# Layer A's third and fourth value projections as seven Strassen products, with sums of x and weights made ahead

## The chip, the cores and the metric

One core of one Trainium2 chip runs the whole program. The metric is the device time of one execution in microseconds (us). The kernel before was timed in 3 runs: median 1818.2 us, from 1813.79 to 1818.61. One more execution was profiled; all durations of instructions come from that one.

## The reference

Two attention layers, A and B, stand side by side; their outputs are concatenated. Each has S = 2048 positions, D = 1024 features, 32 heads of 32, all in float32:

```
qkv = x @ wqkv                      # 2048x1024 @ 1024x3072
q, k, v = heads of qkv
A: each query sees 8 keys, at distances 0, 2, .., 14
B: each query sees the 256 keys up to itself
out = softmax(q k^T / sqrt(32)) v   # per head
return concat(a_out @ wo_A, b_out @ wo_B)
```

The change touches the part `v = x @ wqkv[:, 2048:]` of layer A.

## The kernel before

**Units.** Each layer is cut into 4 units of 512 positions, so there are units 0 to 7. Units 0 to 3 are layer B (dense blocks of scores), units 4 to 7 layer A. Layer A's positions are sorted into even and odd ones first, so a query's 8 keys are neighbours: a window. `U` is 8 and `DU`, the first unit of layer A, is 4.

**Numbers in two parts.** Every operand of the large matrix products is split into a high part, rounded to the matmul's fp32r format, and a low part that holds the rest. A product is three matmuls: high by high, high by low, low by high (`TERMS`). `Stream` loads the operands as a fixed list of items of 512 KB through `NRAW` = 3 landing tiles (`raw`, issued by POOL at line 173), and splits each one: ScalarE or VectorE writes the high part (lines 218 and 221), VectorE the low part (line 224). An item's split sends off the load three items further on.

**Work of one unit.** For each of 8 slots `s` there is one q and one k tile (`qk_items`, line 586: 2 x 8 x 3 = 48 matmuls of 512 columns). Between them stand the value projections (`v_items`, line 654) in three parts (`VPARTS`): part 0 makes the value features of slots 0 to 3 with 96 matmuls of 512 columns; parts 1 and 2 those of slots 4 and 5, and of 6 and 7, with 96 matmuls of 256 columns each. `V_SLOTS` puts the parts behind slots 0, 5 and 7. While part 2 runs, the next unit's x is loaded and split (`x_items`). Values stay in the SBUF tiles `vbuf`, one for each part. Layer B's output projections stand in units 1 to 5 (`o_items`, line 714).

**Output of layer A.** The two units 4 and 5, and then 6 and 7, are taken together, and the output projection over their rows is seven Strassen products instead of eight block products (`product`, line 773, 48 matmuls of 512 columns each): the rows are two halves (the two units), the contraction has two halves, and the outputs have two halves. Sums of blocks are made by `background` tasks: SyncE loads blocks into `r` tiles (line 841), VectorE adds (line 846), SyncE stores the sums to DRAM (line 852), from where `Stream` loads them like any weight. `weight_sums` makes the 4 weight sums of layer A's `wo`, `output_sums` those of the attention outputs `od`.

**Attention of a window.** `window` has two steps on TensorE: scores (line 923) and values (line 984). Between them VectorE masks, takes maxima and sums, and transposes (lines 931 to 961), and ScalarE spreads the result into `wide` (lines 970 and 973). SyncE copies q and k rows into seats in `pbuf` (line 506). PSUM has 3 banks for the large products (`rg`, tiles `g`), 4 for scores (`s`) and 1 for values (`o`).

**What sets the order.** All engines run their instructions in the order in which the program is written. That order comes from a planner in the program: `Clock` keeps estimated times, and the last loop of the function picks from four lists (`aux`, `twos`, `ones`, `gemm`) what can start first. A wait that the planner did not foresee holds everything behind it on that engine.

## Time and profile before

| | |
|---|---|
| median of 3 runs | 1818.2 us |
| profiled execution, whole | 1818.1 us |
| its span, first to last instruction | 1816.4 us |
| TensorE busy | 1789.4 us, 99% |
| VectorE busy | 1262.0 us, 69% |
| ScalarE busy | 924.4 us, 51% |
| mean granted TensorE clock | 0.995 |

The span is 1.7 us shorter than the execution, and the profiled execution is 0.1 us below the median, so a sum made on the trace can be set beside the median as it stands. In the trace, layer A's units 6 and 7 run from about 1337 to 1657 us, and the fourteen output products from 1657 to 1812 us. A busy TensorE in these views is one on which some matmul is under way.

### The profile page before, as it was taken

The numbers are of one execution on the slowest core, as the hardware profiler recorded it, in microseconds if no ns is written. First come the engines' busy times: TensorE is split into PE (matmuls) and PEld (weight loads), VectorE is DVE, ScalarE is ACT, GpSimd is POOL, SyncE is SP. The second block draws the span as 40 slices with busy tenths as digits, with TensorE's granted clock in tenths as the row PEclk, the third lists the DMA queues.
The fourth block names the chain that finished last, engine by engine and source line by source line (L and its number), as shares of the span: only waits on it lengthen the run. The fifth ranks groups of instructions, "written<-read, shape, count | busy, mean of one in ns | idle before, by whom it ended". The sixth has DMA issues, their size and how long they took to land.

```text
span 1816.4 us, 38617 instructions
## 1 busy us (share of the span) xinstructions
PE 1789.4 (99%) x14730; PEld 1465.3 (81%) x14730; DVE 1262.0 (69%) x2790; ACT 924.4 (51%) x2301; POOL 410.1 (23%) x950
## 2 busy tenths in 40 slices
PE   9999999999999999999999999999999999999999
PEld 6787878888777788778887788888888887888887
DVE  6677876768867769777677566646755766557866
ACT  5556466555655565656555344423542544446342
POOL 2313323222242223333224300101010011002220
PEclk9999999999999999999999999999999999999999
DMA  7354664544646555454545343536753674348984
GB/s 239 114 142 136 183 168 139 167 139 137 183 139 177 146 144 170 134 166 128 160 110 164 106 150 119 164 123 213 249 173 113 221 250 137 120 144 297 311 265 145
DMA packets 129241, 303.61 MB, mean 167 GB/s; under 512 B 16160, under 2 KB 31520, under 8 KB 129056
## 3 DMA queue, kind: packets, MB, share of 16 engines
q0 software_dynamic: 45216, 164.65, 28.7%
q1 hardware_dynamic: 73472, 116.56, 22.8%
q10 hardware_dynamic: 10368, 19.93, 3.0%
q8 instruction: 117, 1.92, 0.4%
q14 instruction: 68, 0.56, 0.1%
HBM read 189.79 MB, written 44.04 MB: 129 GB/s over the span
## 4 chain that ended last, share of the span: by engine, by line
PE 91%; DMA 3%; ACT 2%; DVE 2%; issue 1%; SPq 0%; POOL 0%; ACTq 0%; DVEq 0%; POOLq 0%
PE g L586 37%; PE g L654 18%; PE g L714 10%; PE g L773 8%; PE s L1172 5%; PE s L1089 5%; PE o L1219 5%; PE s L923 2%; PE o L984 2%; DMA r<-od 2%; DMA raw<-xs 1%; ACT wide L970 1%; ACT s L1099 0%; DVE w L224 0%; DVE r L846 0%
## 5 line engine op out<-in xcount | busy, mean ns | idle before, releaser
L586 PE MATMUL g<-x,w 128*128 128x512 f32 x3072 | 773.0, 396 | 2.8 <-ACT x L218 2.6
L586 PEld LDWEIGHTS g<-x,w 128*128 128x128 f32 x3072 | 568.1, 189 | 114.5 <-issue 6.8
L654 PE MATMUL g<-w,x 128*128 128x256 f32 (+1 forms) x2304 | 393.7, 322 | 0.5 <-issue 0.3
L224 DVE TENSOR_TENSOR w<-raw,w 128x512 fp32r<-128x512 f32 x518 | 339.4, 697 | 51.8 <-ACT w L218 45.1
L654 PEld LDWEIGHTS g<-w,x 128*128 128x128 f32 x2304 | 334.5, 192 | 28.8 <-issue 1.6
L1099 ACT ACTIVATE s<-s,nm 128x384 f32<-128x384 f32 (+2 forms) x512 | 274.4, 537 | 101.8 <-DVE nm L1094 101.6
L1094 DVE CUSTOM_DVE_ANT_0 s<-s,mask_d 128x384 f32<-128x384 f32 (+2 forms) x512 | 261.7, 554 | 88.1 <-PE s L1089 87.4
L1158 POOL TENSOR_SCALAR_AFFINE_SELECT pbuf<-pbuf 128x128 f32<-128x128 f32 (+1 forms) x606 | 220.1, 391 | 326.2 <-ACT pbuf L1179 324.8
L1179 ACT ACTIVATE pbuf<-s 128x384 f32<-128x384 f32 (+2 forms) x480 | 202.8, 505 | 73.7 <-PE s L1172 72.1
L714 PE MATMUL g<-r,w 128*128 128x512 f32 x768 | 190.8, 394 | 1.4 <-ACT r L1054 0.7
L173 POOL DMA_DIRECT2D raw<-wqk x126 | 68.6, 545 | 440.8 <-DVE w L224 303.0
L714 PEld LDWEIGHTS g<-r,w 128*128 128x128 f32 x768 | 141.9, 188 | 30.7 <-DVE r L1058 1.6
L773 PE MATMUL g<-x,w 128*128 128x512 f32 x672 | 153.2, 390 | 0.5 <-DVE w L224 0.5
L773 PEld LDWEIGHTS g<-x,w 128*128 128x128 f32 x672 | 126.0, 188 | 27.3 <-DVE w L224 0.9
L221 DVE CAST w<-raw 128x1024 fp32r<-128x1024 f32 x187 | 129.3, 692 | 25.2 <-PE g L586 22.6
L1172 PEld LDWEIGHTS s<-qst,kst 128*128 128x128 f32 x704 | 113.3, 189 | 40.6 <-ACT s L1099 16.2
L1089 PE MATMUL s<-kst,qst 96*128 96x384 f32 (+2 forms) x512 | 142.5, 342 | 0.9 <-ACT s L1099 0.7
L1172 PE MATMUL s<-qst,kst 128*128 128x256 f32 (+2 forms) x704 | 136.4, 302 | 3.5 <-ACT s L1099 3.0
L1089 PEld LDWEIGHTS s<-kst,qst 96*128 96x128 f32 x512 | 93.5, 189 | 25.8 <-issue 3.9
L931 DVE TENSOR_TENSOR band<-s,near 128x160 f32<-128x160 f32 x128 | 32.5, 316 | 116.0 <-PE s L923 116.0
L1099 ACT ACTIVATION_READ_ACCUMULATOR s<-s,nm 128x1 f32 x512 | 105.4, 206 | 0.0
L970 ACT COPY wide<-band 32x512 f32<-32x512 f32 x128 | 79.0, 618 | 49.2 <-DVE band L961 47.2
(81 smaller groups left out, 1405.7 us busy)
## 6 DMA issues: line engine op xcount, KB each, us to landing
raw<-wqk POOLq DMA_DIRECT2D x126, 512.0 KB, 4.3
raw<-wv POOLq DMA_DIRECT2D x72, 512.0 KB, 4.9
qst<-nat SPq DMA_DIRECT2D x96, 256.0 KB, 5.4
kst<-nat SPq DMA_DIRECT2D x96, 256.0 KB, 5.5
raw<-wo POOLq DMA_DIRECT2D x44, 512.0 KB, 4.4
raw<-xs POOLq DMA_DIRECT2D x28, 512.0 KB, 4.5
outs<-ost ACTq DMA_DIRECT2D x37, 256.0 KB, 2.8
kst<-halo SPq DMA_DIRECT2D x72, 128.0 KB, 4.4
```

Source lines behind the costliest of these rows:

```text
L221: nc.vector.tensor_copy(t[:, 0, :], raw)
L224: nc.vector.tensor_tensor(t[:, 1, c:c + 512], raw[:, c:c + 512], t[:, 0, c:c + 512].bitcast(F32), op=ALU.subtract)
L586: nc.tensor.matmul(h["ps"], h["w"][:, a, k * P:(k + 1) * P], xt[u][k][:, b, :], start=(k == 0 and i == 0), stop=(k == NK - 1 and i == 2))
L654: nc.tensor.matmul(ps, xt[u][kw * g + k][:, a, p0:p0 + P], h["w"][g][:, c, k], start=(first and t == 0 and half == 0), stop=(last and t == 2),
L714: nc.tensor.matmul(h["ps"], w[:, a, c:c + P], ot[u, k][:, b, :], start=(k == 0 and i == 0), stop=(k == NK - 1 and i == 2))
L773: nc.tensor.matmul(h["ps"], w[:, a, c:c + P], x[:, b, :], start=(k == 0 and t == 0), stop=(k == 3 and t == 2))
L1089: nc.tensor.matmul(ps[:, :n], q[0:96, j, b * P:(b + 1) * P], kk[0:96, j, c0:c1], start=True, stop=True)
L1094: nc.vector.tensor_tensor_reduce(ps[:, :n], ps[:, :n], mask[:, cut:full], scale=-1.0, scalar=BIG, op0=ALU.add, op1=ALU.min, accum_out=nm)
L1099: nc.scalar.activation(ps[:, :n], ps[:, :n], AF.Exp, bias=nm, scale=-1.0, accum_out=sm)
L1158: nc.gpsimd.affine_select(w, w, pattern=[[0, m], [step, n]], compare_op=ALU.is_ge, fill=0.0, base=base, channel_multiplier=chan)
L1172: nc.tensor.matmul(ps[:, i * n:(i + 1) * n], kk[:, j, 256 + kb * P:256 + (kb + 1) * P], q[:, j, q0:q0 + n], start=True, stop=True)
L1179: nc.scalar.activation(w, ps[:, :pack * n].rearrange("p (j n) -> p j n", j=pack), AF.Exp)
```

## The change

Units 6 and 7 (`VPAIR` = 6) no longer run `v_items`. Their value projections, rows of both units against 1024 features and 1024 outputs, become seven products of 48 matmuls of 512 columns (`value_product`), placed by `VP_AT`: products 0 and 1 behind slot 0 of unit 6, 2, 5 and 6 behind slots 1 to 3, 3 behind slot 7, and 4 behind slot 0 of unit 7. The results of unit 6, and part 0 of unit 7, are added straight into `vbuf`. Parts 1 and 2 of unit 7 go to DRAM (`vd`) and come back (`value_load`) once unit 6's attention has freed those tiles.

The products need sums of x blocks and of weight blocks. `half_sums` makes them from unit 3's slot 6 on (`SUMS_FROM` = 30), in 24 steps one after the other through the one tile `slot(3)`: 8 for value weights (`tv`), 8 for x (`sx`), 8 for layer A's `wo` (`td`, in place of `weight_sums`). A step is four loads of 128x256, four additions of 128x256 on VectorE and one store. `Stream` then loads `sx` and `tv` as items. The `background` lanes open only when product 3 is through, so `output_sums` of units 4 and 5 start later.

```diff
+VPAIR = 6
+VP_AT = {(6, 0): (0, 1), (6, 1): (2,), (6, 2): (5,), (6, 3): (6,), (6, 7): (3,), (7, 0): (4,)}
+SUMS_FROM = 30
...
-            if s in vs:
+            if s in vs and u < VPAIR:
                 plan.append(("v", u, vs[s]))
+            plan += [("vp", u, i) for i in VP_AT.get((u, s), ())]
...
+                if kinds[:1] == ["xw"] and k in (0, 2, 4, 6):
+                    st.split_to(then + 1 + k // 2)
...
-                if u == DU - 1 and n == NG - 1:
-                    ck.defer(ck.now + 3.0, weight_sums)
...
+    def value_product(i):
...
+        def run(n, k):
+            if k == 0:
+                h["ps"], h["b"] = rg.take()
+            x, w = left(k)[0], fetch("t", k // 2)[0]
...
+            for t, (y, z) in enumerate(TERMS):
+                nc.tensor.matmul(h["ps"], x[:, y, P * n:P * n + P], w[:, z, k % 2], start=(k == 0 and t == 0),
+                                 stop=(k == 3 and t == 2))
...
+            elif i == 3:
+                e = add(c, c)
...
+                    nc.scalar.dma_start(vd[:, n, :], c)
...
+                e = add(a, a)
+                if n == 3:
+                    bg["idle"] += [0, 1]
+                    ck.defer(ck.now + 3.0, background)
...
+    def value_load(part):
...
+            nc.sync.dma_start(vbuf[part][:, c:c + m, :], vd[:, b:b + m, P * (s0 % 4):P * (s0 % 4 + n)])
...
+    def half_sums(i=0):
...
+        t = slot(3).rearrange("p (a s) -> p a s", a=4)
+        for c in range(4):
+            nc.sync.dma_start(t[:, c, :], loads[c])
+            e = ck.copy("part", ck.now)
+
+        def add():
+            for to, x, y, op in ops:
+                nc.vector.tensor_tensor(*[t[:, c, :] for c in (to, x, y)], op=op)
+                e = ck.use("dve", 0.36, ck.now, port=True)
+            ck.defer(e, put)
+
+        def put():
+            nc.sync.dma_start(dst[:, :, k, 256 * z:256 * z + 256], t)
...
-    bg = {"tasks": [], "idle": [0, 1]}
+    bg = {"tasks": [], "idle": []}
...
+            if VP_AT.get((p[1], NG - 1)) == p[2:] and p[1] + 1 < U:
+                for g, x in reversed(list(enumerate(x_items(p[1] + 1)))):
+                    new[4 * g + XAT:4 * g + XAT] = x
```

In the changed kernel line 586 is line 616, 654 is 691, 923 is 1127, 984 is 1188, 173 is 179, 221 and 224 are 227 and 230, and the new matmuls have line 916, their additions line 931, the half sums' additions line 1025.

Up to unit 3's slot 6 the order on every engine is as it was. Behind it, three places show what moves.

TensorE at the start of unit 6, before: a q and k tile, part 0 of the values (line 654), and attention of windows between (lines 984 and 923).

```order
L586 MATMUL g<-x,w 128x512 x27
L654 MATMUL g<-w,x 128x512 x9
L984 MATMUL o<-wide,vbuf_125 32x8 x4
L984 MATMUL o<-wide,vbuf_125 32x136 x12
L984 MATMUL o<-wide,vbuf_125 32x128 x4
L654 MATMUL g<-w,x 128x512 x36
L923 MATMUL s<-pbuf 32x40 x64
L654 MATMUL g<-w,x 128x512 x51
L586 MATMUL g<-x,w 128x512 x6
```

The same place on TensorE in the changed kernel, and on to product 2 behind slot 1 (`g<-w,r`: its x sums lie in `r` tiles).

```order
L616 MATMUL g<-x,w 128x512 x24
L916 MATMUL g<-w,x 128x512 x21
L1188 MATMUL o<-wide,vbuf_128 32x8 x4
L1188 MATMUL o<-wide,vbuf_128 32x136 x12
L1188 MATMUL o<-wide,vbuf_128 32x128 x4
L916 MATMUL g<-w,x 128x512 x15
L1127 MATMUL s<-pbuf 32x40 x64
L916 MATMUL g<-w,x 128x512 x60
L616 MATMUL g<-x,w 128x512 x6
L1188 MATMUL o<-wide,vbuf_126 32x136 x12
L1188 MATMUL o<-wide,vbuf_126 32x128 x4
L616 MATMUL g<-x,w 128x512 x42
```

The 96 matmuls of part 0 have given way to 96 of products 0 and 1; the same attention steps stand between them.

POOL's queue of loads from unit 6's last slots into unit 7, before: q and k weights, part 2's value weights, then unit 7's x with the weights around it.

```order
L173 DMA raw<-wqk 128x1024 x4
L173 DMA raw<-wv 128x1024 x2
L173 DMA raw<-wqk 128x1024
L173 DMA raw<-xs 128x1024 x4
L173 DMA raw<-wqk 128x1024
L173 DMA raw<-wv 128x2x512 x5
```

The same place in the changed kernel: product 3's four items (x sums and weight sums in turn) stand ahead of unit 7's x, product 4's weight sums behind it.

```order
L179 DMA raw<-wqk 128x1024 x8
L179 DMA raw<-sx 128x1024
L179 DMA raw<-tv 128x1024
L179 DMA raw<-sx 128x1024
L179 DMA raw<-tv 128x1024
L179 DMA raw<-wqk 128x1024
L179 DMA raw<-xs 128x1024 x4
L179 DMA raw<-wqk 128x1024
L179 DMA raw<-tv 128x1024 x2
```

A product takes four items where part 2 took two, just ahead of the four items of x.

VectorE at the switch to unit 7, before: low parts of unit 7's x (line 224), and a window's softmax (lines 943 to 961).

```order
L943 TENSOR_TENSOR band<-band,nm 128x16x40
L224 TENSOR_TENSOR w<-raw,w 128x512 x4
L224 TENSOR_TENSOR x<-raw,x 128x512 x4
L955 TENSOR_REDUCE sm<-band 128x16
L957 RECIPROCAL sm<-sm 128x16
L959 TENSOR_TENSOR band<-band,sm 128x16x40
L961 STREAM_TRANSPOSE band<-band 128x1024
L224 TENSOR_TENSOR x<-raw,x 128x512 x4
```

The same place on VectorE in the changed kernel, with the last half sum (line 1025) and product 3's additions (line 931) among them.

```order
L230 TENSOR_TENSOR x<-raw,x 128x512 x2
L1025 TENSOR_TENSOR r<-r 128x256 x4
L931 TENSOR_TENSOR r<-g,r 128x512 x2
L230 TENSOR_TENSOR x<-raw,x 128x512 x2
L931 TENSOR_TENSOR r<-g,r 128x512 x2
L1159 TENSOR_REDUCE sm<-band 128x16
L1161 RECIPROCAL sm<-sm 128x16
L1163 TENSOR_TENSOR band<-band,sm 128x16x40
L1165 STREAM_TRANSPOSE band<-band 128x1024
L230 TENSOR_TENSOR x<-raw,x 128x512 x2
L931 TENSOR_TENSOR r<-g,r 128x512 x2
L230 TENSOR_TENSOR x<-raw,x 128x512 x2
```

The additions that free PSUM banks now wait their turn between x's low parts and behind a half sum, whose loads must have landed.

More of the change, by code (lines that the diff above doesn't have):

```diff
@@ L280 @@
     td = dram.tile([P, 4, 4, S], F32, name="td")
+    tv = dram.tile([P, 4, 4, S], F32, name="tv")
+    sx = dram.tile([P, 4, 4, S], F32, name="sx")
+    vd = dram.tile([P, 4, S], F32, name="vd")
     done = {}
-    for k in ("stack", "v", "o", "ot", "out", "nat", "second", "clear", "scores", "s", "t"):
+    for k in ("stack", "v", "o", "ot", "out", "nat", "second", "clear", "scores", "s", "t", "vs", "vw", "vd"):
         done[k] = {}
@@ L356 @@
     st.gates = gates
+    firsts = {where["vp", i, "t", 0] for v in VP_AT.values() for i in v}
     where_o = {"ot": 0, "s": 0, "bg": 0}
@@ new lines, in value_load @@
+    def value_load(part):
+        u = VPAIR + 1
+        s0, n = VPARTS[part]
+        if (u, part) in done["v"] or len(done["vd"]) < 4 or \
+                any((u - 1) * NG + s not in done["o"] for s in range(s0, s0 + n)):
+            return
+        b = 0
+        while b < 4:
+            c = (4 * u + b) % 6
+            m = min(4 - b, 6 - c)
+            nc.sync.dma_start(vbuf[part][:, c:c + m, :], vd[:, b:b + m, P * (s0 % 4):P * (s0 % 4 + n)])
+            e = ck.copy("load", ck.now)
+            b += m
+        done["v"][u, part] = e + VNEED
@@ new lines, in half_sums, with end @@
+    def half_sums(i=0):
+        if i == 24:
+            return
+        k, z = i % 8 // 2, i % 2
+        if i < 8:
+            w = wv[units[VPAIR][0]].rearrange("(j t i) p c -> j t i p c", j=2, t=2)
+            loads = [w[c // 2, z, c % 2, :, 256 * k:256 * k + 256] for c in range(4)]
+            ops, dst, key, who = WEIGHT_OPS, tv, "vw", (k, z)
+        elif i < 16:
+            loads = [xs[VPAIR + c // 2][:, k + c % 2 * 4, 256 * z:256 * z + 256] for c in range(4)]
+            ops, dst, key, who = OUTPUT_OPS, sx, "vs", (k, z)
+        else:
+            loads = [wo[units[DU][0], k + c // 2 * 4, :, S * (c % 2) + 256 * z:S * (c % 2) + 256 * z + 256] for c in range(4)]
+            ops, dst, key, who = WEIGHT_OPS, td, "t", (k, z)
+        t = slot(3).rearrange("p (a s) -> p a s", a=4)
[9 more added lines that the diff above has]
+            nc.sync.dma_start(dst[:, :, k, 256 * z:256 * z + 256], t)
+            e = ck.copy("load", ck.now)
+            def end():
+                done[key][who] = ck.now
+                st.load_to(st.wanted)
+                half_sums(i + 1)
+            ck.defer(e + VREST, end)
+        ck.defer(e + BG_SLACK, add)
@@ L1029, in finish @@
         done["o"][hg] = ck.now
+        if u == VPAIR:
+            for p in (1, 2):
+                value_load(p)
+        if hg == SUMS_FROM:
+            half_sums()
         if u >= DU:
-            o = slot(2 + hg % 2)[:, :S]
+            if "o" not in fin:
+                fin["o"] = slot(2)
+            o = fin["o"][:, S * (hg % 2):S * (hg % 2) + S]
             nc.scalar.copy(o, h["o"])
```

140 lines of the change are left out of this document (126 added, 14 removed).

## Prediction

> **What bounds the kernel now.** I read the page's busy times and its chain first, then what TensorE waits for, then the busy times of three stretches. Of the page, the span, the engines and the chain that ended last, by engine and by line:
>
> ```profile
> span 1816.4 us, 38617 instructions
> PE 1789.4 (99%) x14730; PEld 1465.3 (81%) x14730; DVE 1262.0 (69%) x2790; ACT 924.4 (51%) x2301; POOL 410.1 (23%) x950
> PE 91%; DMA 3%; ACT 2%; DVE 2%; issue 1%; SPq 0%; POOL 0%; ACTq 0%; DVEq 0%; POOLq 0%
> PE g L586 37%; PE g L654 18%; PE g L714 10%; PE g L773 8%; PE s L1172 5%; PE s L1089 5%; PE o L1219 5%; PE s L923 2%; PE o L984 2%; DMA r<-od 2%; DMA raw<-xs 1%; ACT wide L970 1%; ACT s L1099 0%; DVE w L224 0%; DVE r L846 0%
> ```
>
> TensorE is idle for 27.0 of 1816.4 us, and the chain is TensorE's own queue nearly from end to end. Time that its queue loses is time that the kernel loses, unless a wait grows in its place. The waits of TensorE's queue (in total, how many, the longest), cut to those that matter below, show how few there are:
>
> ```profile
> PE o L984 <- ACT wide L973: 3.8, 3, 2.5
> PE o L984 <- issue: 2.6, 1, 2.6
> PE o L984 <- DVE vbuf L610: 0.9, 1, 0.9
> PE g L773 <- DVE w L224: 0.5, 1, 0.5
> ```
>
> Busy times of the stretches in which the change works: from unit 3's slot 6 to the start of unit 6, units 6 and 7, and the output products. Columns: length, then busy time and count of each engine, granted clock, DMA share, GB/s.
>
> ```profile
> 1030.00:1337.20 307.20, 304.35 (x3896) 253.77 (x3895) 185.22 (x312) 124.02 (x233) 32.56 (x59) 1.00 0.52 169
> 1337.20:1657.40 320.20, 312.60 (x4011) 261.78 (x4009) 199.63 (x338) 140.98 (x268) 33.76 (x59) 0.99 0.53 171
> 1657.40:1812.40 155.00, 154.44 (x716) 126.95 (x712) 114.54 (x187) 63.41 (x93) 27.82 (x49) 1.00 0.77 264
> ```
>
> TensorE is full in all three. VectorE has 39% of the first two to spare (185.2 and 199.6 busy of 627.4 us), and the 16 DMA engines nearly half.
>
> **Term 1, TensorE's work.** The large products' matmuls in units 6 and 7 by shape, and the page's row of the output products, whose form the value products copy:
>
> ```profile
> L586 PE MATMUL g<-x,w 128*128 128x512 f32 x746 | 177.1, 396 | 0.0
> L654 PE MATMUL g<-w,x 128*128 128x256 f32 x384 | 48.0, 286 | 0.0
> L654 PE MATMUL g<-w,x 128*128 128x512 f32 x192 | 45.1, 392 | 0.0
> L773 PE MATMUL g<-x,w 128*128 128x512 f32 x672 | 153.2, 390 | 0.5 <-DVE w L224 0.5
> ```
>
> The mean of one, 390 ns, is a latency; busy time divided by count is the price, since matmuls overlap. All of the old value work goes: 48.0 + 45.1 = 93.1 us. Seven products of 48 matmuls of 512 columns, 336, come. In the same stretch one costs 45.1 / 192 = 0.235 us (attention cuts in between), so 78.9 us; at the output products' undisturbed 153.2 / 672 = 0.228 us it would be 76.6 us. I take the first, since the new products stand among the same attention steps: **-14.2 us**, with -16.5 as the other end. Nothing else of TensorE's work changes: q, k, scores, values and output products keep their counts. That the 256-column form is no bargain is in the rows (48.0 / 384 = 0.125 us, a little over half of 0.235).
>
> **Term 2, starts of the products.** A value part asks for an item at a time, or two; a product with sums needs all four (two of x, two of weights) at its start, with three landing tiles. The new order: the fourth load goes off during the fourth of eight steps of the first tile of q and k before, and its split stands in the fourth step of the second tile, 24 matmuls or 5.6 us later. How long POOL's loads take from issue to landing in units 6 and 7, what ScalarE's split takes, and VectorE's low parts:
>
> ```profile
> DMA to landing us min/median/max: 3.4/4.8/11.0
> L218 ACT CAST w<-raw 128x1024 fp32r<-128x1024 f32 (+1 forms) x73 | 75.3, 1037 | 45.0 <-DVE band L791 12.9 <-DVE r L791 7.6 <-PE g L654 7.2
> L224 DVE TENSOR_TENSOR w<-raw,w 128x512 fp32r<-128x512 f32 x98 | 63.1, 686 | 24.0 <-ACT w L218 22.9
> ```
>
> Split and two low parts take 1.04 + 2 x 0.69 = 2.4 us; the first matmul that reads them is about 20 matmuls, 4.7 us, behind the split. So a load of up to 5.6 + 4.7 - 2.4 = 7.9 us costs nothing, the median has 3 us in hand, and only the far tail of 11.0 would stall TensorE, by 3.1 us. Bounds for five such starts: 0 and 15.5. The nearest row is TensorE's wait at the first output product, 0.5 us: 5 x 0.5 = **+2.4 us**. Products 0 and 1 use x and weights as they are and start like a value part.
>
> **Term 3, the half sums.** 24 steps, each with four additions of 128x256, run from 1030 us until product 3, some 440 us. A 128x256 addition isn't in the trace. Rows on both sides of it, the second with what it waited for, then the additions that read a PSUM bank, and VectorE's wait on the loads of a sum:
>
> ```profile
> L931 DVE TENSOR_TENSOR band<-s,near 128x160 f32<-128x160 f32 x64 | 16.2, 315 | 51.1 <-PE s L923 51.1
> L846 DVE TENSOR_TENSOR r<-r 128x512 f32<-128x512 f32 x24 | 16.6, 692 | 18.7 <-DMA r<-od 18.1
> L791 DVE TENSOR_TENSOR r<-g,r 128x512 f32<-128x512 f32 x40 | 26.8, 687 | 21.6 <-PE g L773 21.6
> DVE r L846 <- DMA r<-od: 18.1, 5, 8.3
> ```
>
> Between 0.32 and 0.69 us; I take half of the second, 0.35: 96 x 0.35 = 34 us (66 at the upper end), less 16 x 0.69 = 11 of the weight sums that go. The products' additions are 24 of 512 columns and 8 of 256, 24 x 0.69 + 8 x 0.35 = 19 us, against 4 copies (3 us) saved. VectorE gains some 39 us (up to 71) on 384.9 of 627.4: 67%, at most 73%. The output products ran at 114.5 of 155 us, 74%, and TensorE lost half a microsecond there. So the work itself is hidden.
>
> Each step moves 1.05 MB, 25.2 MB in all, less 8.4 MB of the old weight sums; 4 more items and the trip of the values add 4.2. The price per MB from the row of SyncE's queue (packets, MB, share of the 16 engines' span):
>
> ```profile
> q1 hardware_dynamic: 73472, 116.56, 22.8%
> 1237.00:1300.00 63.00, 63.00 (x899) 53.22 (x901) 42.17 (x72) 24.19 (x46) 4.22 (x8) 1.00 0.74 246
> ```
>
> 22.8% of 1816.4 us for 116.56 MB is 3.55 us of all 16 engines per MB. The half sums' 25.2 MB are 89 us, or 20 points on a share of 0.52 over 440 us: 0.72. The second row is the stretch with the old weight sums: share 0.74, and TensorE busy for 63.00 of 63.00 us. I price the traffic at **0**. Behind a half sum's store, on SyncE, stand the copies of q and k rows into their seats; on VectorE, behind its first addition, low parts and bank releases. Both wait as long as its loads are late; the second rival prices that.
>
> **Terms at nothing.** The values' trip through DRAM (4 stores on ScalarE, 4 loads on SyncE) is issued four slots ahead of its first reader, over 40 us, against landings of 4.0 us for a store of 256 KB:
>
> ```profile
> od<-r SPq DMA_DIRECT2D x32, 256.0 KB, 4.0
> ```
>
> Without that cover it would cost one landing, 4 us. The sums of units 4 and 5 begin at the end of unit 6 instead of in it, and are wanted some 180 us later. One more window's attention falls among the output products; its TensorE time moves and stays the same. The x of unit 7 is loaded under product 3 instead of under part 2; product 3 reads sums alone, so x tiles come free earlier, but four more loads stand ahead on POOL's queue. I leave that switch as it is: 0, bounds in the first and third rivals.
>
> **Sum.** 1818.1 - 14.2 + 2.4 = 1806.3 us. The profiled execution is 0.1 us below the median of 1818.2, so the sum stands for the median.
>
> **The price of a stall** is more than its length. TensorE at the switch to unit 7 and in unit 7's last slots, as a timeline, and two stretches around them:
>
> ```profile
> 1500.88 1.50 PE L984 MATMUL o<-wide,vbuf 128*32 128x136 f32 x32 [2.54 <-ACT wide L973]
> 1502.32 3.75 PE L586 MATMUL g<-x,w 128*128 128x512 f32 x10
> 1599.64 0.64 PE L984 MATMUL o<-wide,vbuf 128*32 128x136 f32 x11 [2.55 <-issue]
> 1498.00:1506.00 8.00, 5.46 (x45) 0.79 0.38 118
> 1598.00:1606.00 8.00, 6.36 (x41) 0.79 0.06 19
> ```
>
> After an idle stretch of 2.54 us ten matmuls take 3.75 us instead of 2.35, and the mean clock over the 8 us is 0.79: 0.21 x 8 = 1.7 us lost on top. The stall of 2.55 us put down to issue, which ends at 1599.64, has the same trail in the last row. [...]
>
> **Rivals.** Two timeline rows for the second, of VectorE and TensorE shortly before the output products, and the weight sums of unit 5 as a group:
>
> ```profile
> 1652.08 2.87 DVE L846 TENSOR_TENSOR r<-r 128x512 f32<-128x512 f32 x4 [3.34 <-DMA r<-od]
> 1656.81 0.66 PE L984 MATMUL o<-wide,vbuf 128*32 128x136 f32 x16 [0.90 <-DVE vbuf L610]
> L846 DVE TENSOR_TENSOR r<-r 128x512 f32<-128x512 f32 x16 | 11.0, 688 | 0.4
> ```
>
> - *The two stalls of units 6 and 7 go* (they hung on late x under part 2, and on nothing that the profile shows). For: product 3 needs no x tile, and the stall at 1597 has no cause in the program that the profile shows. Against: x still lands through three tiles, behind four more loads. Gain 2.54 + 2.55 + 2 x 1.7 = 8.5 us: 1797.8; at the -16.5 end and with no wait at the starts, 1793.1.
> - *Half sums hold VectorE, and TensorE starves; slower.* Place: line 1025 in VectorE's queue, 24 times. In the trace five of eight background sums held VectorE, 18.1 us in total, 3.6 each, and after the one of 3.34 us TensorE waited 0.9 us for values in `vbuf`. If each of the 24 did that: 24 x 0.9 = 21.6, so 1818.1 - 14.2 + 21.6 = 1825.5 us. It decides from 14.2 / 24 = 0.6 us of TensorE per step. Against: the four weight sums (last row, 1237 to 1300 us), also between windows, held VectorE for 0.4 us in all, and a half sum's loads are a quarter in size.
> - *Product starts stall.* Loads in the tail meet the half sums' traffic: three of five starts wait 3.1 us and lose 1.7 us of clock, 14.4 us: 1818.3, no gain.
> - *The work isn't less*: excluded, since the order has 240 matmuls fewer (336 for 576).
>
> **How the numbers follow.** Forecast, from 1801 to 1811: 0.60. The stalls go, 1793 to 1801: 0.16. Starts stall, 1811 to 1823: 0.16. Half sums starve TensorE, above 1823: 0.08. The range from 1796 to 1815 leaves out the last (0.08), about half of the third and the far end of the second. A measurement can tell about 0.3% (5.5 us) from no change, so faster means under 1812.7: the first two and a little of the third, 0.79; within it 0.13; slower 0.08.
>
> **What the profile after would show.** Line 916 with 336 matmuls at 77 to 79 us and TensorE busy near 1775 us; waits of line 916 for low parts (line 230) under 1 us each; VectorE's waits at line 1025 short; stretch 1030 to 1337 unchanged in length. Wrong would be waits of 2 us or more at line 916, 1188 or 616 with half-clock stretches behind, a longer stretch before unit 6, or a matmul of line 916 far from 0.235 us.

## The result and the profile after

The changed kernel takes 1827.5 us (median of 6 runs), the kernel before 1816.9 us on the same chip (6 runs): a ratio of 1.0057, with a 95% interval from 1.0039 to 1.0076. It is slower, where 1806.3 us was forecast. The profiled execution of the changed kernel took 1823.9 us, its span is 1822.2 us; it is one of the shorter of its runs, and the profiled execution of the kernel before is 1.2 us above its median, so the traces show 5.8 us of a difference that is 10.6 us in the medians.

The changed kernel's page, span, engines and bytes moved:

```profile
span 1822.2 us, 38428 instructions
PE 1783.0 (98%) x14490; PEld 1445.0 (79%) x14490; DVE 1306.1 (72%) x2901; ACT 931.0 (51%) x2309; POOL 416.0 (23%) x955
DMA packets 154650, 324.58 MB, mean 178 GB/s; under 512 B 18016, under 2 KB 58976, under 8 KB 154464
```

TensorE's 240 matmuls fewer are there, but it is busy only 6.4 us less (1789.4 before), and idle for 39.2 us instead of 27.0. Where the time lies shows in three stretches, each cut at the same matmuls of q and k: units 4 and 5, unit 6, and unit 7 with the output products. First the kernel before, then the changed one (length, then busy time and count of PE, PEld, DVE, ACT and POOL, clock, DMA share, GB/s):

```profile
959.40:1337.20 377.80, 374.34 (x4311) 308.24 (x4310) 233.38 (x432) 162.56 (x341) 59.62 (x118) 1.00 0.50 159
1337.20:1492.70 155.50, 153.88 (x1970) 129.31 (x1969) 100.86 (x176) 70.83 (x134) 16.57 (x30) 1.00 0.60 195
1492.70:1812.40 319.70, 313.15 (x2754) 259.42 (x2752) 213.31 (x349) 133.56 (x228) 45.01 (x79) 0.99 0.61 204
```

```profile
959.80:1345.00 385.20, 377.56 (x4310) 309.62 (x4309) 244.74 (x474) 164.86 (x344) 62.24 (x119) 1.00 0.57 176
1345.00:1529.70 184.70, 176.10 (x1970) 141.34 (x1969) 131.79 (x244) 81.05 (x149) 22.46 (x40) 1.00 0.65 198
1529.70:1817.40 287.70, 280.67 (x2513) 226.56 (x2512) 214.52 (x351) 126.86 (x218) 40.80 (x72) 0.99 0.74 252
```

Length less busy time is TensorE's idle time. It rose from 3.5 to 7.6 us in units 4 and 5, where TensorE's work is the same, and from 1.6 to 8.6 us in unit 6; behind that it stayed (6.6 and 7.0). From unit 6 to the end TensorE's busy time fell from 467.0 to 456.8 us. So the stretch in which the products stand gained 2.8 us, where the prediction has a gain of 11.8, and the stretch ahead of it lost 7.4. The stop shown below, and the half clock behind it, make 4.0 of these 7.4.

The matmuls of the products in the changed kernel, and waits of TensorE's queue (total, how many, longest): those of layer A's windows and all of line 916:

```profile
L916 PE MATMUL g<-w,r 128*128 128x512 f32 x192 | 46.6, 395 | 2.3 <-DVE r L931 0.8 <-DVE nat L523 0.8 <-ACT w L224 0.7
L916 PE MATMUL g<-w,x 128*128 128x512 f32 x144 | 36.7, 409 | 2.7 <-DVE w L230 1.5 <-DVE nat L523 0.8 <-ACT w L224 0.5
```

```profile
PE s L1127 <- issue: 7.4, 4, 3.7
PE o L1188 <- ACT wide L1177: 3.8, 4, 1.2
...
PE o L1188 <- issue: 2.3, 1, 2.3
...
PE g L916 <- DVE nat L523: 1.6, 2, 0.8
...
PE g L916 <- DVE w L230: 1.5, 1, 1.5
PE s L1127 <- DMA pbuf<-nat: 1.4, 3, 0.9
PE g L916 <- ACT w L224: 1.2, 2, 0.7
PE g L916 <- DVE r L931: 0.8, 1, 0.8
```

The two waits put down to `nat L523` end with low parts of weights too: that line is a memset of 0.07 us, which VectorE runs right behind them.

The largest group waits for nothing that the profile shows: 9.7 us put down to issue, 4.8 before, the rows of which are:

```profile
PE o L984 <- issue: 2.6, 1, 2.6
PE s L923 <- issue: 1.9, 2, 1.4
PE g L654 <- issue: 0.3, 1, 0.3
```

One of these stops in full, before and after, as timelines:

```profile
1155.22 1.28 PE L923 MATMUL s<-pbuf 32*32 32x40 f32 x124
1157.92 0.26 PE L923 MATMUL s<-pbuf 32*32 32x40 f32 x4 [1.41 <-issue]
```

```profile
1157.52 1.30 PE L1127 MATMUL s<-pbuf 32*32 32x40 f32 x126
1162.52 0.29 PE L1127 MATMUL s<-pbuf 32*32 32x40 f32 x2 [3.70 <-issue]
```

Two stretches of the changed kernel around half clock, behind this stop and behind a wait of product 4:

```profile
1160.00:1168.00 8.00, 5.49 (x28) 5.09 (x28) 6.51 (x14) 4.20 (x8) 1.45 (x2) 0.79 0.46 147
1546.00:1554.00 8.00, 6.97 (x24) 5.61 (x25) 7.79 (x12) 1.50 (x2) 0.53 (x1) 0.79 0.80 265
```

TensorE stops in the middle of one window's scores, four matmuls from the end before and two in the changed kernel. The longer stop also leaves a half clock behind it: the granted clock is 0.50 from 1163 to 1165 us, a mean of 0.79 over 8 us, 1.7 us of work. So does the wait: 0.50 from 1549 to 1551 us.

### The profile page after: what moved, and what is told of

It is laid out like the page before. It is cut to its first block, busy times and chain, and to the rows that moved or that the text cites. A ratio compares the mean times of both kernels' runs of the same rounds, so it can differ in the third digit from the quotient of the medians.

```text
span 1822.2 us, 38428 instructions
## 1 busy us (share of the span) xinstructions
PE 1783.0 (98%) x14490; PEld 1445.0 (79%) x14490; DVE 1306.1 (72%) x2901; ACT 931.0 (51%) x2309; POOL 416.0 (23%) x955
## 5 line engine op out<-in xcount | busy, mean ns | idle before, releaser
L230 DVE TENSOR_TENSOR w<-raw,w 128x512 fp32r<-128x512 f32 x510 | 334.8, 698 | 57.0 <-ACT w L224 50.7
L691 PE MATMUL g<-w,x 128*128 128x256 f32 (+1 forms) x1728 | 301.3, 323 | 0.2 <-DVE w L230 0.2
L691 PEld LDWEIGHTS g<-w,x 128*128 128x128 f32 x1728 | 252.4, 192 | 19.7 <-DVE w L230 0.9
L808 PEld LDWEIGHTS g<-x,w 128*128 128x128 f32 x672 | 126.6, 189 | 27.4 <-ACT w L224 0.5
L227 DVE CAST w<-raw 128x1024 fp32r<-128x1024 f32 x181 | 125.4, 693 | 7.1 <-PE g L616 3.0
L224 ACT CAST w<-raw 128x1024 fp32r<-128x1024 f32 (+1 forms) x75 | 77.7, 1040 | 71.5 <-PE g L916 28.1
L1174 ACT COPY wide<-band 32x512 f32<-32x512 f32 x128 | 79.1, 618 | 44.1 <-DVE band L1165 37.4
```

What stands on the lines that cost most here:

```text
L227: nc.vector.tensor_copy(t[:, 0, :], raw)
L230: nc.vector.tensor_tensor(t[:, 1, c:c + 512], raw[:, c:c + 512], t[:, 0, c:c + 512].bitcast(F32), op=ALU.subtract)
L691: nc.tensor.matmul(ps, xt[u][kw * g + k][:, a, p0:p0 + P], h["w"][g][:, c, k], start=(first and t == 0 and half == 0), stop=(last and t == 2),
L808: nc.tensor.matmul(h["ps"], w[:, a, c:c + P], x[:, b, :], start=(k == 0 and t == 0), stop=(k == 3 and t == 2))
```

## The experiments

All ratios are to the kernel before, on the same chip; runs of one batch (same first letter) share it. A difference of two ratios is uncertain by some 0.002, 3 to 4 us.

| run | median us | ratio, 95% interval |
|---|---|---|
| the changed kernel | 1827.5 | 1.0057, 1.0039 to 1.0076 |
| e1_products_no_sums | 1822.8 | 1.0031, 1.0017 to 1.0045 |
| e2_sums_no_products | 1824.8 | 1.0039, 1.0024 to 1.0054 |
| e3_output_weight_sums_only | 1819.4 | 1.0016, 1.0006 to 1.0027 |
| e4_sum_traffic_no_adds | 1827.8 | 1.0060, 1.0045 to 1.0075 |
| c1_after_shift32 | 1821.1 | 1.0033, 1.0022 to 1.0044 |
| c2_after_shift80 | 1844.5 | 1.0158, 1.0137 to 1.0180 |
| c3_before_shift32 | 1822.1 | 1.0027, 1.0014 to 1.0039 |
| c4_after_lanes_late | 1823.5 | 1.0040, 1.0025 to 1.0055 |
| d1_lanes_late_shift104 | 1820.3 | 1.0020, 1.0009 to 1.0030 |
| d2_products_no_sums_late_shift104 | 1813.9 | 0.9991, 0.9980 to 1.0003 |
| d3_late_shift104_values_later | 1813.7 | 0.9988, 0.9975 to 1.0002 |
| f1_late_values_later_no_shift | 1816.7 | 1.0007, 0.9998 to 1.0017 |
| f2_sums_denser | 1806.3 | 0.9955, 0.9941 to 0.9969 |
| f3_before_shift64 | 1818.1 | 1.0020, 1.0009 to 1.0031 |
| g1_after_sums_denser | 1817.6 | 1.0005, 0.9991 to 1.0019 |
| g2_sums_denser_late_values_later | 1807.1 | 0.9950, 0.9931 to 0.9969 |
| g3_sums_denser_no_products | 1816.9 | 1.0004, 0.9993 to 1.0015 |
| h1_no_products_values_later | 1813.5 | 0.9993, 0.9982 to 1.0004 |

### Each half of the change alone

e1: the products, with plain blocks in place of sums. It leaves out the 16 steps for x and value weights, so its values are not the reference's.

```diff
-                item(key, "xw", sx[:, a, 2 * j:2 * j + 2, :])
+                item(key, "xw", xs[VPAIR + a % 2][:, 2 * j:2 * j + 2, :])
...
-            half_sums()
+            half_sums(16)
```

> The changed kernel without the 16 half-sum steps for x and the value weights: the products load plain blocks of x and weights of the same size in place of the sums (so units 6 and 7 of the output come from blocks that are no sums); the 8 steps for the output weights stay. Theory A (the traffic and the queue places of the half sums cost the time, before unit 6 above all): the 7 to 8 us lost ahead of unit 6 come back, and a part of the losses in units 6 and 7, so 1808 to 1815 us. Theory B (the products' own demand for items in units 6 and 7 costs it): 1822 to 1828 us, as the changed kernel.

e2, e3, e4: the value parts, and the opening of the background lanes, as before. e2 makes all 24 half sums, e3 only the last eight (those of `wo`), e4 all, but the first 16 without the additions.

```diff
-VP_AT = {(6, 0): (0, 1), (6, 1): (2,), (6, 2): (5,), (6, 3): (6,), (6, 7): (3,), (7, 0): (4,)}
+VP_AT = {}
...
-            for to, x, y, op in ops:
+            for to, x, y, op in ops if i >= 16 else ():
```

> All 24 half-sum steps, but the values by the old parts in all units; the sums of x and value weights are made and not used. Theory A: 6 to 10 us above the same kernel with the 8 output-weight steps alone, 1823 to 1828 us. Theory B: within 2 us of that kernel.

> The old value parts, and only the 8 half-sum steps for the output weights (which took the place of the four larger weight sums). Both theories: within 2 us of the kernel before, 1815 to 1819 us. It is the base for the other two.

> As the kernel with all 24 steps and the old value parts, but the 16 steps for x and value weights load and store without the additions on VectorE (what they store is no sum and is not used). If it is the traffic (theory A as stated): the same as with the additions, 1823 to 1828 us. If it is VectorE's queue held by additions that wait for loads: 1816 to 1819 us. Theory B: 1815 to 1819 us.

Adding the 16 new steps costs 0.0023, 4 us (e2 against e3), with products 0.0026, 5 us (the changed kernel against e1). Without their additions they cost no less (e4). A part of e4's time is stops: 11.3 us put down to issue, against 7.4 in e2 and 6.9 in e3. TensorE's other waits add up to 18.8 us in e4, 19.0 in e2 and 16.8 in e3, so e4 stands with e2 there too. So VectorE's work in the 16 steps is not what costs. And the products alone gain nothing that shows: e1 is 0.0015 above e3, less than a difference can tell.

The traces show where the cost lies, and it is not beside the 16 steps. These run in units 4 and 5 (their loads are issued from 975 to 1338 us in the changed kernel), and there the pairs are equal: 384.1 us in e2 and 384.9 in e3, 385.2 in the changed kernel and 385.3 in e1. But the steps go one after the other, so the 16 push the eight steps for `wo` back: their loads are issued from 973 to 1156 us in e1, e3 and d2 (d1 without its 16 steps, below), and from 1358 to 1524 us in e2, the changed kernel and d1. Behind that the pairs part: unit 6 takes 184.7 us in the changed kernel and 179.1 in e1, 186.3 in d1 and 182.3 in d2; e2 and e3 reach unit 7's q and k at 1496.8 and 1496.7 us and part behind it. So the likely price is one of the late place of eight steps that e1 and e3 have as well. This is argued, not shown: in e4 the eight stand earlier (loads from 1296 to 1463 us), and it is no faster, with its stops. And e4 keeps the additions of these eight, so it doesn't tell whether their transfers, their additions or the order that the planner makes around them cost the time. No run takes these apart.

### Stops that belong to a place in the code

The stop of the timelines above came at matmul 7892 to 7896 of TensorE's stream in all six profiles up to here, 1.41 to 4.23 us long. The queue of instructions, q8, in the kernel before (14730 matmuls) and in the changed one (14490), packets and MB:

```profile
q8 instruction: 117, 1.92, 0.4%
```

```profile
q8 instruction: 115, 1.88, 0.4%
```

That is 16 KB for every 126 matmuls (115 and 117 pieces, where the expectation of c1 has 113 to 115), each of which is a weight load and a multiplication. If TensorE stops because the next such piece isn't there, the stop must move when the stream is shifted. c1 to c3 and f3 put cheap matmuls among those at the very start: 32 in c1 and c3, 80 in c2, and in f3, as in d1 to d3 and f2, matmuls of 32x32 in float32, each of which shows as two in the trace (with 52 of them d3 and f2 have 14594 matmuls, the changed kernel 14490; c4, in the same batch, is told below). c1's edit:

```diff
+        for i in range(32):
+            nc.tensor.matmul(ps[:, :32], idle[:, :P], idle[:, :32], start=True, stop=True)
         ck.free["pe"] = 0.6 + 0.43 * WARM
```

> The changed kernel with 32 extra matmuls of 32 columns among the warm-up matmuls at the very start; nothing else differs, so every later TensorE instruction stands 32 matmuls later in TensorE's own instruction stream. Theory C (code): queue q8 brings TensorE's instructions in pieces of 16 KB, one for every 128 matmuls (113 to 115 pieces for 14490 to 14730 matmuls); a window's 128 score matmuls use a whole piece up in 1.3 to 3 us, and TensorE stops in the middle of a group where the next piece is late. The stop sits at the same matmul in all six profiles so far (number 7892 to 7896 of the stream: 1.41 us before, 2.6 to 4.2 us in the five others). With the shift it must be gone from that matmul (now 7926), and the sum of idle time put down to issue falls from 9.7 to about 5 us, since fewer score groups end a piece: 4 to 6 us less than the changed kernel, 1821 to 1823.5 us. Rival (the stops are bound to the traffic of that moment or to a wait that the profile doesn't show): the stop stays at its place in the program, and the time stays at 1826 to 1829.

> The same with 80 extra matmuls of 32 columns. Theory C: at this shift seven instead of four score groups of units 4 to 7 use a piece up in under 2 us; the stop leaves its old matmul too, but others come, so idle put down to issue is 9 us or more, and the time 1826 to 1832 us. Rival: the stop stays at its place, 1826 to 1829, with the same list of stops as in the changed kernel.

> The kernel before with 32 extra matmuls of 32 columns at the start: the control. Theory C: the stops at matmuls 7892 and 13209 (1.41 and 2.55 us) leave their places; three score groups instead of four use a piece up in under 2 us, so the time is the same or up to 4 us less: 1813 to 1818 us. Rival (stops belong to place or moment): both stops stay, 1817 to 1818.

> The kernel before with 32 extra matmuls of 32x32 in float32 at the start (64 in the trace): the worst position by the trace of before, with eight pieces of code used up in under 2 us instead of four. Nothing else differs. Theory C: more stops, at matmuls that are 64 apart from where the model puts them in before (6752, 9287, 9540, 10679, 11058, 11816, 12322, 12829): 5 to 10 us slower than before. Rival (position is a matter of a microsecond or two): 1814 to 1818, with stops at 7956 and 13273, the places of before.

In all four the stops left their instructions. c1's timeline where the changed kernel stopped for 3.70 us (the whole group of 128 now runs through), and where it now stops:

```profile
1156.81 1.31 PE L1127 MATMUL s<-pbuf 32*32 32x40 f32 x128
...
1512.95 0.90 PE L1188 MATMUL o<-wide,vbuf 128*32 128x136 f32 x22
1517.28 0.61 PE L1188 MATMUL o<-wide,vbuf 128*32 128x136 f32 x10 [3.43 <-issue]
```

The new stop is at matmul 11818. From the old one, 7894, that is 31 pieces of 126.6 matmuls. Over the profiles of before, after and all 18 runs there are 64 such stops of 0.7 us or more behind matmul 5800. They fall on 24 places, and 61 of them within 6 matmuls of a grid of 126.6. The count of q8's packets gives nearly the same: 14490 / 115 = 126.0 matmuls for one.

The traces hold the time of each packet of q8, and these show the release itself. In the changed kernel the stop of 3.70 us begins at 1158.81 us, the next piece is on its way from 1159.93 to 1161.06 us, and TensorE goes on at 1162.52, 1.45 us behind the landing. All 64 stops end 1.2 to 1.6 us behind the landing of a 16 KB packet of q8. Of TensorE's 121 other waits of that length two do, and they end anywhere from 0.1 to 17.5 us behind one. So that the stops are waits for code is shown.

Which end of a piece stops isn't settled: of the eight places that the expectation of f3 names, one stopped (9284), and two other places did; d1 was to have 4 us of issue or less and has 6.5. The size came out otherwise than expected too: c1 gained 0.0024, as expected, but its stops still add up to 9.1 us; c3 lost 0.0027 where 0 to 4 us of gain was expected, and f3 lost 0.0020, less than expected. c2's total says nothing: its 80 matmuls delayed the start by 10 us, which its expectation left out; from unit 4 on it is 11 us above the changed kernel. In c1, c3 and f3 the position is a draw of 4 to 5 us either way, for the kernel before too.

### Order and place

c4 opens the background lanes behind product 4, d1 adds a shift of 104, d2 takes the sums out of d1 (as e1), d3 has the planner count ScalarE's spreads as done 1.3 us later in units 6 and 7, f1 is d3 without the shift.

```diff
-                if n == 3:
-                    bg["idle"] += [0, 1]
-                    ck.defer(ck.now + 3.0, background)
             else:
                 e = add(seat(0, 1), a)
                 known(u + 1, 0)
+                if n == 3:
+                    bg["idle"] += [0, 1]
+                    ck.defer(ck.now + 3.0, background)
...
-            return latest(done["v"].get((u, vp)), h.get("p"), ro.when())
+            p = h.get("p")
+            return latest(done["v"].get((u, vp)), p and u >= VPAIR and p + 1.3 or p, ro.when())
```

> The changed kernel, but the background lanes (the sums of units 4 and 5's outputs) open when product 4 is through, not product 3. Theory S (switch): at the switch to unit 7 their four loads of 512 KB, x of unit 7, the items of products 3 and 4 and the last half sums stand in the DMA engines together (share 0.94 and 0.95 from 1520 to 1560 us), and product 4 waits for its weights (1.47 and 0.5 us) and pays for it with half clock; later lanes take these waits away: 3 to 5 us less than the changed kernel, 1822.5 to 1824.5. Theory C alone: the stops put down to issue stay, and the switch gives 1 us at most: 1826 to 1828. Should the sums now be late for the output products, they show as waits on r<-od at the end of unit 7 and the time rises.

> The changed kernel with late lanes (as in c4_after_lanes_late) and 52 extra matmuls of 32x32 in float32 at the start, each of which shows as two in the trace: a shift of 104. Theory C (code pieces): worked out from the trace of c4_after_lanes_late, with its stream shifted by 104, one piece is used up in under 2 us instead of four, and 3 instead of 4 in under 3 us. So the stops at matmuls 7894, 10300 and 13589 (3.38, 1.42 and 3.50 us) are gone, idle time put down to issue falls from 9.8 to 4 us or less, and with the half clock behind two of them the kernel takes 7 to 9 us less than c4_after_lanes_late: 1814 to 1817 us, a little faster than the kernel before. Rival (code position is worth no more than the 4 us of a lucky draw): 1820 to 1824.

> As d1_lanes_late_shift104, but products read plain blocks of x and weights in place of sums (as in e1_products_no_sums; the values are not the reference's), and only the eight steps for wo remain of the half sums. Theory C alone: the sums' traffic costs only by making late pieces of code later, so without stops it costs little: within 2 us of d1. Rival (the sums cost by queues and transfers whatever the code does): 4 to 6 us less than d1, as e3 against e2.

> As d1_lanes_late_shift104, and in units 6 and 7 the planner counts ScalarE's spreads as done 1.3 us later than before, so that a window's value matmuls are put behind some more matmuls of q and k or of a product. Theory P (planner): the three waits of 1.15, 1.20 and 1.22 us on ScalarE's spreads, which stand at the same places in three profiles of the changed kernel (at 1422, 1447 and 1474 us), come from estimates of VectorE and ScalarE that are 1.2 us short; they go, and the time falls by 2.5 to 4 us against d1. Rival (those waits are filled by something else late, such as a PSUM bank): within 1 us of d1. The changed order also moves code pieces by a few matmuls, which may bring a stop of 2 to 3 us back.

> As d3_late_shift104_values_later without the extra matmuls at the start, which makes the table of four complete: late lanes alone (c4), with the shift (d1), with the later values (this), with both (d3). Theory C: worked out from d3's trace, three instead of one piece of code are used up in under 2 us (at matmuls 7996, 9136 and 10402), so stops of 2 to 3.5 us with a half clock behind them come back: 1816 to 1820 us, 2.5 to 6 above d3. Theory P alone: what d3 gained over d1 (6.7 us) all came from the later values, and this kernel stands within 2 us of d3: 1812 to 1816.

Late lanes: 0.0017, about 3 us, within what the pair can show. The shift to the best position: 0.0020 (c4 to d1), half of what theory C gave it there, and 0.0019 (f1 to d3), within what it gave. The later values: 0.0033 (c4 to f1) and 0.0032 (d1 to d3), 6 us, more than the three waits of 1.2 us. Taking out the 16 steps: 0.0029 (d1 to d2), 5 us, the third pair to say so, and not within 2 us as theory C alone had it.

### The pace of the half sums

The planner leaves 6 us between two steps, so that the last one stands at 1523 us, beside unit 7's x. f2 and g1 to g3 leave 2 us; the last additions are then over at 1407 to 1409 us.

```diff
-VREST, VLAST, VNEED = 6.0, 2.0, 3.0
+VREST, VLAST, VNEED = 2.0, 2.0, 3.0
```

f2 is d3 with this edit, g1 the changed kernel with it, g2 f1 with it, g3 e2 with it; h1 is g3 with the later values, the control for g2.

> As d3_late_shift104_values_later, but the pause that the planner leaves between two half sums is 2 us instead of 6, so that the last of the 24 should be over at about 1430 us, not 1520, and no longer meets x of unit 7 and the items of products 3 and 4 at the switch. Theory S (switch): the waits there (1.67 and 0.89 us at line 616, 0.89 at line 1189, from 1531 to 1537 us) shrink, 1 to 3 us less than d3: 1811 to 1813. Rival T (the sums cost by their transfers wherever they stand): the same bytes in less time make other loads late earlier, in units 4 and 5, and the time is the same or up to 4 us more: 1813 to 1818.

> The changed kernel with one edit: a pause of 2 us instead of 6 between two half sums, so that the last one is over near 1410 us, before the switch to unit 7. Lanes, values and code position are those of the changed kernel. Theory T' (the sums cost where they stand among other late loads, from the second half of unit 6 on): most of what f2 gained over d3 (7.4 us) comes here too: 1819 to 1823. Theory C alone (f2 gained because its code pieces happened to fit): the stops at 7894 and 13590 stay, and the time is within 2 us of the changed kernel: 1825 to 1829.

> As f2_sums_denser without the 52 matmuls at the start: late lanes, later values, denser sums, at the code position of the changed kernel. Theory C: by f2's trace three short pieces instead of none, the stop at 7894 (3.1 to 4.2 us in seven runs) and a half clock come back: 1810 to 1814, 4 to 8 above f2. Rival: position is worth no more than f1 against d3 (3 us): 1806 to 1810.

> As e2_sums_no_products (all 24 half sums, value parts as in the kernel before) with a pause of 2 us instead of 6. Theory T': the 16 sums cost e2 5.4 us over e3 because their last steps met the switch to unit 7 and the loads behind it (the tables of e2 and e3 are equal up to the switch, 1496.8 and 1496.7 us); with the sums over by then the ratio to the kernel before falls from 1.0039 to 1.0010 to 1.0020, as e3. Theory T (transfers cost wherever they stand): it stays at 1.0035 or more.

> The control for g2_sums_denser_late_values_later: g3_sums_denser_no_products (all half sums, dense, value parts as before) with the planner's later values in units 6 and 7. If the products are what makes g2 fast, this stays at g3's ratio of 1.0004, give or take 0.0015. If the later values give g2 its gain whatever the values are made by, it falls to 0.997 or less.

This one number is worth 0.0052 in the changed kernel (g1), 0.0035 without products (g3), 0.0033 and 0.0057 in d3 and f1 (f2, g2): 6 to 10 us in four pairs. f2, g1 and g3 came out below the ranges that their expectations give. In the traces 1.1 to 3.7 us of each gain lie in units 4 and 5, where less is put down to issue; the larger part lies in unit 6 with products (3.0 to 8.3 us), and behind it without them (5.0 us), where the pairs above part. All 24 half sums at the denser pace cost no more than eight at the old one (g3 against e3): the last eight are then loaded from 1268 to 1401 us, some ahead of unit 6 and the rest in its first half. The position of the code made no difference then (f2, g2), against theory C. g2's page:

```profile
span 1801.9 us, 38465 instructions
PE 1776.0 (99%) x14490; PEld 1440.8 (80%) x14490; DVE 1304.3 (72%) x2896; ACT 934.6 (52%) x2314; POOL 414.5 (23%) x955
DMA packets 154651, 324.59 MB, mean 180 GB/s; under 512 B 18016, under 2 KB 58976, under 8 KB 154464
```

Its matmuls of the products:

```profile
L916 PE MATMUL g<-w,r 128*128 128x512 f32 x192 | 46.1, 394 | 0.2 <-DVE w L230 0.2
L916 PE MATMUL g<-w,x 128*128 128x512 f32 x144 | 33.8, 392 | 0.0
```

Its three stretches:

```profile
955.93:1339.12 383.19, 377.08 (x4310) 309.63 (x4309) 253.44 (x494) 165.36 (x345) 62.21 (x119) 1.00 0.61 189
1339.12:1515.88 176.76, 175.41 (x1970) 141.44 (x1969) 124.51 (x226) 77.87 (x146) 22.90 (x41) 1.00 0.59 181
1515.88:1798.20 282.32, 278.42 (x2513) 225.38 (x2511) 209.73 (x345) 133.38 (x225) 40.59 (x72) 0.99 0.76 256
```

It moves the same bytes as the changed kernel, with the same matmuls, and its span is 20 us shorter. Its idle time in unit 6 is 1.4 us instead of 8.6, and the products wait for next to nothing. g1, with the pace alone, already has 2.1 us there:

```profile
1340.59:1517.73 177.14, 175.09 (x1970) 141.65 (x1969) 121.75 (x222) 80.86 (x149) 22.37 (x40) 1.00 0.59 181
1517.73:1814.18 296.45, 283.69 (x2513) 228.64 (x2511) 213.96 (x350) 129.27 (x221) 40.54 (x72) 0.98 0.72 244
```

Its second row has 12.8 us of idle time. A third of it is product 4's wait for its weights, with lanes and x beside them, which is gone in g2 with its late lanes; the row is from g1's waits:

```profile
PE g L916 <- DVE w L230: 4.2, 2, 4.0
```

In e2 and g3, without products, the pace shows in the transfers of 1410 to 1530 us, first e2:

```profile
1410.00:1530.00 120.00, 116.31 (x1637) 97.00 (x1636) 88.13 (x158) 59.20 (x112) 12.63 (x22) 1.00 0.80 255
```

```profile
1410.00:1530.00 120.00, 118.55 (x1530) 100.45 (x1523) 86.47 (x148) 58.62 (x110) 13.15 (x23) 1.00 0.66 215
```

What stays open is which queue carries the cost. The expectation of f2 named three waits at the switch (1.67, 0.89 and 0.89 us); in f2 they are still 1.67, 0.38 and 0.72 us, so it gained 0.7 us there, and more by stops (4.8 to 1.2 us of issue in all) and small waits elsewhere. In each of the four pairs the dense run has less issue (1.2 to 6.3 us; 4.8 to 13.8 in the runs with all 24 sums at the old pace), but a free DMA engine is not what they gain. Four microseconds around the stop at matmuls 7891 to 7894, in g3, which stopped for 1.43 us, and in the changed kernel, which stopped for 3.70 us:

```profile
1151.00:1155.00 4.00, 2.57 (x138) 2.31 (x138) 1.68 (x3) 2.21 (x4) 0.09 (x1) 1.00 1.01 374
```

```profile
1156.00:1160.00 4.00, 2.81 (x140) 2.54 (x139) 2.44 (x5) 1.31 (x3) 0.53 (x1) 1.00 0.97 351
```

The DMA share is full in both. Nor is it the total time for which the half sums hold VectorE: that was longer at line 1025 in g2 than in the changed kernel, here first the changed kernel, then g2:

```profile
L1025 DVE TENSOR_TENSOR r<-r 128x256 f32<-128x256 f32 x96 | 40.7, 424 | 37.1 <-DMA r<-wo 10.6 <-DMA r<-xs 8.6 <-issue 8.5
```

```profile
L1025 DVE TENSOR_TENSOR r<-r 128x256 f32<-128x256 f32 x96 | 41.0, 427 | 42.7 <-DMA r<-xs 21.5 <-DMA r<-wv 16.2 <-DMA r<-wo 2.6
```

What the holds of the last eight steps alone cost in unit 6 these rows don't tell.

Part of it is the planner: in the changed kernel and in e1 the scores of 19 windows stand ahead of unit 6's slot 3, in g1 and g2 those of 18. That the pace moves windows in this way is seen; that it is why the waits on spreads went is only argued, and it can't be all: e2 and g3 both have 18, and the pace gained 0.0035 there. A moved window also moves code, so the pace and the position of the code are not fully apart in these pairs.

The products themselves: h1 against g2 is 0.0043, 8 us. Of g2's 9 us, some 2 may come from the later values, since h1 gains 0.0011 over g3 by them, which is less than the pair can tell.

## Why the prediction was wrong, point by point

- **What bounds the kernel** was right: TensorE's queue. Each loss found is a wait or a stop on it, or the clock behind one.
- **Term 1** (-14.2 us) was nearly right, once the waits are gone: in g2 line 916 takes 46.1 + 33.8 = 79.9 us, forecast 78.9, and TensorE is busy for 1776.0, forecast near 1775. In the changed kernel it takes 83.3, part of it at half clock, and busy time from unit 6 on fell by 10.2 us.
- **Term 2** (+2.4 us) was mis-sized: line 916 waited 5.0 us, twice the value taken and a third of the upper bound, and the half clock at 1548 us behind product 4's wait adds 1.7. In g2, with dense sums, late lanes and later values, it is 0.2 us: the waits were not the starts' own, but those of their loads among others.
- **Term 3** is the step that failed: "I price the traffic at 0". With the 16 new steps the kernels took 4 to 5 us more in three pairs, and the pace of all 24 is worth 0.0052, 9 us, in the changed kernel itself. In these pairs the time was lost from unit 6 on, to where the 16 push back the eight steps for `wo`, and not in units 4 and 5, where the 16 move their bytes. The work on VectorE was nearly right: the additions took 40.7 us, forecast 34, with 424 ns for one in place of 350, and VectorE was busy 44.1 us longer, forecast 39. The row behind it, share 0.74 with TensorE full, was a stretch without x, items of products or lanes beside it; a share says nothing of what stands in the queue ahead of a late load. That this queueing is the mechanism is argued, not shown; which queue carries it stays open. And the price is not one of the bytes: at another pace the same bytes cost nothing that shows.
- **Terms at nothing**: "I leave that switch as it is: 0". Lanes opened behind product 3 met x and product 4 there; opened later they gave some 3 us (c4), no more than the pair can show, and 10 us together with later values at the denser pace (g1 to g2).
- **Not in the sum at all**: the stops at ends of code pieces, taken as unexplained and constant. They doubled from 4.8 to 9.7 us. A change that takes 240 matmuls out moves every later instruction against the ends of the pieces. But the largest growth stands ahead of unit 6, where no matmul was taken out: the same stop, within two matmuls, took 3.70 us instead of 1.41, and 3.14 with the eight sums for `wo` alone (e3). The prediction named a longer stretch before unit 6 as a sign of being wrong; this stop with its half clock is more than half of it.
- **The rivals**: "half sums hold VectorE, and TensorE starves" gave 1825.5 us, close to the time, but it has each of the 24 steps cost 0.9 us, and the 16 in units 4 and 5 cost nothing that shows (e2 against e3, e4); the nearness is luck. For the last eight it isn't excluded. It shows once, and small: the additions of line 931 at 1524 us ran behind the last half sum, and TensorE waited 0.85 us. "The two stalls go": the one at the switch did, the other, a stop for code, came back elsewhere. "Product starts stall" took three waits of 3.1 us, each with a half clock; the longest was product 4's, 2.0 us in two parts, and it alone had one behind it.
- **The range**, 1796 to 1815, was too narrow by what wasn't priced: chance of slower 0.08, with the hidden traffic put at exactly 0 and no upper end worked out for it. g2, with the pace, the lanes and the values changed, stands at 0.9950, which on the kernel before's 1816.9 us is 1807.8, near the forecast: what was missed is the schedule around the products, not their work.

## What to carry to other kernels

Work put under a full engine isn't free because busy shares leave room: ask of each background transfer which late load, on which queue, it stands beside, when it is over, and what it pushes back behind it; here a pause of 2 us in place of 6, with the lanes and the values moved, turned 0.6% slower into 0.5% faster. When an engine stops in the middle of a group for no wait that the profile shows, look whether the stop keeps its place in the instruction stream, and whether a packet of the instruction queue lands just before its end, here 1.2 to 1.6 us before, at all 64 stops: then look at the code, and shift it, as the 32 matmuls of c1 did, which moved the stop of 3.70 us away. Judge a change of under 1% by several versions of its schedule, since the position of the code alone moved this kernel by 4 to 5 us.

## What the runs showed of the hardware

TensorE's code came in pieces of 16 KB, one for 126.6 matmuls. At the ends of some pieces (61 of 64 stops stood within 6 matmuls of a grid of 126.6) TensorE stopped for 0.7 to 4.2 us, 53 times of 64 among a window's scores or values, and each time it went on 1.2 to 1.6 us behind the landing of a piece. In the changed kernel half clock (0.50) began behind the stop of 3.70 us (at 1162.5 us), behind waits of 0.51 and 1.47 us in a row (at 1548.2 us) and behind a stop of 2.30 us (at 1657.4 us); each of the three stretches lasted 3.4 us and cost 1.7. In d1 it came behind a stop of 1.63 us (1618 us); in c4 a stop of 3.50 us (1651 us) had none behind it.
